# Quarters of the values projection placed between the groups of transposed rows, in a four-layer attention and feed-forward kernel

## The chip, the cores and the metric

The kernel runs on one core of a Trainium2 chip. The metric is device time in microseconds (us) of one execution. The time before is 1589.06 us, the median of three runs (1588.38 to 1591.19).

## What is computed

The input is 2048 rows of 640 numbers. Two kinds of layers alternate, twice each: sliding-window attention (32 heads of 20, a window of 256 rows) and a feed-forward layer with a squared ReLU.

```python
x = x + _A_ref(_layernorm(x, axis=-1), A_wqkv, A_wo)
x = x + _B_ref(_layernorm(x, axis=-1), B_w1, B_b1, B_w2, B_b2)
x = x + _A_ref(_layernorm(x, axis=-1), A_wqkv, A_wo)
x = x + _B_ref(_layernorm(x, axis=-1), B_w1, B_b1, B_w2, B_b2)

# in _A_ref: H = 32, Dh = 20, W = 256
scores = jnp.einsum("bhqd,bhkd->bhqk", q, k) * (Dh ** -0.5)
mask = (idx[:, None] - idx[None, :] >= 0) & (idx[:, None] - idx[None, :] < W)
p = _softmax(jnp.where(mask[None, None], scores, -1e9), axis=-1)
o = jnp.einsum("bhqk,bhkd->bhqd", p, v)          # then @ wo
# in _B_ref: h = max(x @ w1 + b1, 0) ** 2, out = h @ w2 + b2
```

## The kernel before

**Units.** The 2048 rows are cut into 8 groups of 256; a *unit* u is one group in one attention-and-feed-forward pair, so there are 16 units. A unit needs its normalised rows transposed (`yT`), the projections to queries and keys (`stage_qk`) and to values (`stage_v`), eight *quads* of four heads each of attention, the output projection (`stage_o`) and the feed-forward part (`stage_f`). Numbers are carried as two float16 halves, so that a product takes three matmuls; `mm3` at L330 issues nearly all of the dense ones.

**Normalising and transposing.** `ln_load(u)` loads two blocks of 128 rows into `xt` (L431, on SyncE's queue) and normalises them: statistics on VectorE (L356, L360, L361), a power on GpSimd (L367), the scaling on VectorE (L369). For units 0 to 2 `ln_t(u)` then transposes the blocks on TensorE: `split_t` takes a block as two groups, of three and of two transposes (L404), each group into one PSUM bank, from which ScalarE takes the high half (L390) and VectorE the low half (L391). The values are projected in four quarters (two blocks by two halves of the columns), each of 15 matmuls of 128x320 (L330), evicted by ScalarE (L597).

**PSUM.** Dense accumulators, transposes and the values' products (`pv`) share two banks (`mm_tile`, tag `mm`, two buffers), so that the third such piece of work has to wait until one of the two before it has been evicted. The scores have six banks of their own (`bb`).

**Queries and keys.** Ten groups of 15 matmuls of 128x256 (L330), five for the queries, then five for the keys. They are evicted in pairs by ScalarE (L523) and VectorE (L526) into one buffer `qd`, written to DRAM when queries or keys are complete (L559, L561), and read back in another layout into `qt` and `kt` (L565). There is one `qd` for units 1 and 2: the keys' first eviction waits until the write of the queries has landed.

**A quad of attention.** I write m0 to m7 for unit 0's eight quads of maximum scores (L686; from unit 1 on L671, m8 and up), whose row maxima VectorE takes (L652). After each two quads TensorE transposes the maxima (L739), VectorE splits them (L744, L745) and SyncE's queue writes them as rows of `qt` with four DMAs (L707); I call the four such steps r0, r1, r2, r3. Then come s0, s1, ...: the scores once more with the maxima in them (L783, from s9 on L775), whose exponentials ScalarE takes (L797) and GpSimd masks (L812, L816); and v0, v1, ...: the product with the values (L846), copied out (L858) and written to DRAM (L863).

**What sets the order.** Every engine's order is fixed when the program is built: `tc.manual_schedule` takes instructions as they are recorded. TensorE's order is that of the code; work for the other engines is posted with an estimated cost and a rank (`post`, a lower `prio` first) and recorded by `pump` when a clock of estimates says that it can start. In unit 0 `flow` goes through a list of m, r, s and v steps; wherever the next step's inputs are not yet there by the estimates, it takes pieces of dense work from the generator `ahead_all`, which holds the projections of units 0 to 2 that come ahead of the loop. The estimates know when a row maximum or an exponential is ready; that `qd` is still being read by a DMA they do not know. `convert` turns weights into two halves on ScalarE (L259) and VectorE (L260); the weights are loaded by DMAs that ScalarE issues (L288, L297, L312).

```python
    def split_t(y, dst, m, job, made, bb=None):
        for k, (c0, n) in enumerate(((0, 3), (3, 2))):
                tr, jobs = mm_tile([P, 4, P], "tr")
    def ahead_all():
        yield from stage_qk(0)
    todo = [("m", n) for n in range(GQ)] + [("r", 0)] + [("m", n) for n in range(GQ, LEAD)]
    for n in range(NQ):
        todo += [("s", n)] + ([("r", n + LEAD - GQ)] if n % GQ == 1 else []) + [("m", n + LEAD), ("v", n)]
    flow(todo, rest)
```

Of the kernel before, what the change touches and what calls it, by code (L numbers as in the profile page):

```python
# [16 lines left out]
P = 128  # L17
# [28 lines left out]
def kernel(ctx: ExitStack, tc: tile.TileContext, x, wqkv, wo, w1, b1, w2, b2, out):  # L46
# [86 lines left out]
    def post(eng, cost, fn, *deps, wait=0.0, prio=1, **kw):  # L133

        j = Job(eng, cost, fn, [d for d in deps if d is not None], now[0] + wait, prio, **kw)
        k = len(pend)
        while k and pend[k - 1].prio > prio:
            k -= 1
        pend.insert(k, j)
        return j  # L140
# [5 lines left out]
    def dma(fn, size, *deps, n=1, cost=450.0, prio=1, **kw):  # L146

        return post("S", n * cost, fn, *deps, prio=prio, size=size, **kw)
# [18 lines left out]
    def need(*js):  # L167

        for j in js:
            while j.end is None:  # L170
                pass_time()
            now[0] = max(now[0], j.end)
# [55 lines left out]
    def mm_tile(shape, name):  # L228


        while len(banks2) > 1:
            empty = [b for b in banks2 if b and all(j.end is not None for j in b)]
            if empty:
                b = min(empty, key=lambda b: max(j.end for j in b))
                now[0] = max(now[0], max(j.end for j in b) + LAT)
                banks2.remove(b)
            else:
                pass_time()
        t = ps.tile(shape, F32, name=name, tag="mm", bufs=2)
        banks2.append([])  # L240
        return t, banks2[-1]
# [80 lines left out]
    def mm3(acc, lhs, rhs, nk, ns, then=None, whole=0):  # L322

        k, t = 0, 0.0
        terms = ((0, 0), (0, 1), (1, 0))
        if whole:
            terms = [[t] for t in (terms if whole == 1 else terms[::2] + terms[1:2])]
        for c, part in ([(c, part) for part in terms for c in range(nk)] if whole else [(c, terms) for c in range(nk)]):
            for a, b in part:
                nc.tensor.matmul(acc, lhs(a, c), rhs(b, c), start=(k == 0), stop=(k == 3 * nk - 1))  # L330
                k += 1
                t += ns
                if t >= STEP and k < 3 * nk:
                    yield t
                    t = 0.0
        if then is not None:
            then(t)
        yield t
# [10 lines left out]
    def layernorm(src, y, *deps, prio=2):  # L349

        box = {}

        def stats(i):
            if i == 0:
                box["st"] = sb.tile([P, 2, 6], F32, name="bst", bufs=2)
            nc.vector.bn_stats(box["st"][:, i, :], src[:, i * HD:(i + 1) * HD])  # L356

        def var():
            box["mv"] = mv = sb.tile([P, 4], F32, name="bmv", bufs=2)
            nc.vector.bn_aggr(mv[:, 0:2], box["st"])  # L360
            nc.vector.tensor_scalar(mv[:, 2:3], mv[:, 1:2], 1e-5, YS ** -2, op0=ALU.add, op1=ALU.mult)  # L361

        j = None
        for i in range(2):
            j = post("D", 455, lambda i=i: stats(i), j, *(deps[i:i + 1] or deps), prio=prio)
        j = post("D", 400, var, j, prio=prio)
        j = post("G", 520, lambda: nc.gpsimd.tensor_tensor(box["mv"][:, 3:4], box["mv"][:, 2:3], neghalf,  # L367
                                                                   op=ALU.pow), j, prio=prio)
        j = post("D", 576, lambda: nc.vector.tensor_scalar(y, src, box["mv"][:, 0:1], box["mv"][:, 3:4],  # L369
                                                           op0=ALU.subtract, op1=ALU.mult), j, prio=prio)  # L370
        return j

    def halves(tile):

        return lambda a, c, n, m: tile[:, a, c:c + n, m]

    def pieces_of(*tiles):

        return lambda a, c, n, m: tiles[2 * a + c // 3][:, c % 3:c % 3 + n, m]

    ALL = slice(0, T)

    def split_t(y, dst, m, job, made, bb=None):


        yield Want(job, bank=False)
        need(job)

        def out(tr, jobs, c0, n, wait):
            j = post("A", 170 * n, lambda: nc.scalar.copy(dst(0, c0, n, m), tr[:, :n]), wait=wait, prio=0)  # L390
            j = post("D", 170 * n, lambda: nc.vector.tensor_sub(dst(1, c0, n, m), tr[:, :n], dst(0, c0, n, m)), j,  # L391
                     prio=0)
            jobs.append(j)
            made.append(j)

        parts = []
        for k, (c0, n) in enumerate(((0, 3), (3, 2))):
            if bb is not None:
                tr, jobs = bb[:, k].rearrange("p (c n) -> p c n", n=P), bbjobs
            else:  # L400
                yield Want()
                tr, jobs = mm_tile([P, 4, P], "tr")
            for c in range(n):
                nc.tensor.transpose(tr[:, c, :], y[:, (c0 + c) * P:(c0 + c + 1) * P], ident)  # L404
            parts.append((tr, jobs, c0, n, 117 * n if bb is None else 117 * KC))
            if bb is None:
                out(*parts.pop())
                yield 117 * n
        if parts:
            for p in parts:  # L410
                out(*p)
            yield 117 * KC
# [3 lines left out]
    def xsrc(l, b):  # L416
        return x_rows[b * P:(b + 1) * P, :] if l == 0 else xs[b]
# [7 lines left out]
    def ln_load(u, *deps, prio=2):  # L425

        l, g = divmod(u, NG)
        ys = []
        for i in range(2):
            xt = sb.tile([P, D], F32, name="xt", tag="xt", bufs=2)  # L430
            load = dma(lambda xt=xt, i=i: nc.sync.dma_start(xt, xsrc(l, 2 * g + i)), P * D * 4, *deps, prio=min(prio, 1))  # L431
            ys.append((xt, layernorm(xt, xt, load, prio=prio)))
        lns[u] = ys

    def ln_t(u, yT=None):
        ys = lns.pop(u)
        if u == 0:
            yT = pieces_of(sb.tile([P, 3, T], F16, name="yT", tag="yT", bufs=1), sb.tile([P, 2, T], F16, name="rs", bufs=1),
                           *[sb.tile([P, n, T], F16, name="x1", bufs=2) for n in (3, 2)])
        else:  # L440
            yT = halves(sb.tile([P, 2, KC, T], F16, name="yT", tag="yT", bufs=1) if yT is None else yT)
        yTs[u], pre[u] = yT, []
        bb = banks() if u == 0 else (None, None)
        for i in range(2):
            yield from split_t(ys[i][0], yT, slice(i * P, (i + 1) * P), ys[i][1], pre[u], bb[i])

    def cross(ys, dst, room, prio=2):

# [34 lines left out]
    pre = {}  # L483
# [100 lines left out]
    def stage_v(u, which=range(4)):  # L584
        yT = yTs[u]
        for i in range(2):
            if u == 2:
                yield Want(sums[i], bank=False)
            vt = vts[(2 * u + i) % 6][0]
            for h in range(2):  # L590
                if 2 * i + h not in which:
                    continue
                yield Want()
                acc, jobs = mm_tile([P, 2 * T], "acc")
                need(*[wqj[c] for c in range((2 * D + h * HD) // P, (2 * D + (h + 1) * HD - 1) // P + 1)])
                def out(vt=vt, acc=acc, h=h):
                    nc.scalar.activation(vt[:, h * NP:(h + 1) * NP, 0:DH],  # L597
                                                 acc[:, :HD].rearrange("p (h d) -> p h d", d=DH),
                                                 AF.Copy, scale=1.0 / (YS * WS))

                yield from mm3(acc[:, :HD], lambda a, k: yT(a, k, 1, slice(i * P, (i + 1) * P)),
                               lambda b, k: wq_s[:, b, k, 2 * D + h * HD:2 * D + (h + 1) * HD], KC, 136,
                               lambda wait: jobs.append(post("A", 320, out, wait=wait, prio=urgency["out"])))
# [11 lines left out]
    def banks():  # L615
        need(*bbjobs)
        bbjobs.clear()
        return bb6
# [252 lines left out]
    x1s, ys, y2s = {}, {}, {}  # L871
# [357 lines left out]
    place = kts[2].rearrange("p a n -> p (a n)")[:, :2 * KC * T].rearrange("p (a c n) -> p a c n", a=2, n=T)  # L1229

    def ahead_all():
        yield from stage_qk(0)
        yield from stage_v(0, range(2))
        yield from ln_t(1, place)
        ln_load(2)
        yield from stage_v(0, range(2, 4))
        yield from stage_qk(1)
        yield from ln_t(2)
        yield from stage_v(1)
        gate2.end = now[0]  # L1240
        yield from stage_qk(2)
        yield from stage_v(2)
# [65 lines left out]
```

## Time and profile before

| | |
|---|---|
| median of three runs | 1589.06 us |
| the profiled execution's own time | 1596.68 us |
| its span, first to last instruction | 1595.0 us |
| TensorE busy | 1561.6 us (98%) |
| VectorE busy | 983.5 us (62%) |
| ScalarE busy | 734.0 us (46%) |
| GpSimd busy | 601.1 us (38%) |
| mean granted TensorE clock | 0.993 |

The profile is of one execution, which took 7.62 us more than the median of the runs that were timed without it; 1.68 us of its time lie outside the span. PE is TensorE's matmuls, PEld its weight loads, DVE VectorE, ACT ScalarE, POOL GpSimd, SP SyncE; ACTq and SPq are the instructions with which ScalarE and SyncE issue DMAs. In a timeline a row reads: start in us, length in us, engine, line, operation, out<-in, count, and in brackets the idle time ahead of it and what ended that. PEclk is the granted clock of TensorE as a share of full speed. Line numbers are those of the kernel before; in the changed kernel all from L409 on are higher by two.

### The profile page before, as it was taken

The numbers are of one execution on the slowest core, as the hardware profiler recorded it, in microseconds if no ns is written. First come the engines' busy times: TensorE is split into PE (matmuls) and PEld (weight loads), VectorE is DVE, ScalarE is ACT, GpSimd is POOL, SyncE is SP. The second block draws the span as 40 slices with busy tenths as digits, with TensorE's granted clock in tenths as the row PEclk, the third lists the DMA queues.
The fourth block names the chain that finished last, engine by engine and source line by source line (L and its number), as shares of the span: only waits on it lengthen the run. The fifth ranks groups of instructions, "written<-read, shape, count | busy, mean of one in ns | idle before, by whom it ended". The sixth has DMA issues, their size and how long they took to land.

```text
span 1595.0 us, 52003 instructions
## 1 busy us (share of the span) xinstructions
PE 1561.6 (98%) x21302; PEld 1169.1 (73%) x21302; DVE 983.5 (62%) x3253; ACT 734.0 (46%) x1593; POOL 601.1 (38%) x1291
## 2 busy tenths in 40 slices
PE   8889999999999999999999999999999999999999
PEld 7666767777777777777777777777777777776767
DVE  8777655666656667565466656557665665756441
ACT  4455535345454444535444453444545345454522
POOL 1233525335253343524324252442535235353512
PEclk9998999999999999999999999999999999999999
DMA  9754254453434524344352534535344353431120
GB/s 282 193 164 117 63 120 82 98 119 67 118 90 101 113 54 119 86 120 94 88 130 65 122 87 112 101 78 119 70 123 83 97 122 64 110 83 57 29 67 17
DMA packets 243207, 160.41 MB, mean 101 GB/s; under 512 B 91160, under 2 KB 226712, under 8 KB 242968
## 3 DMA queue, kind: packets, MB, share of 16 engines
q1 hardware_dynamic: 236600, 147.58, 38.5%
q10 hardware_dynamic: 6368, 9.50, 2.1%
q8 instruction: 167, 2.74, 0.7%
q14 instruction: 72, 0.59, 0.1%
HBM read 84.68 MB, written 52.95 MB: 86 GB/s over the span
## 4 chain that ended last, share of the span: by engine, by line
PE 91%; DVE 3%; DMA 2%; ACT 2%; issue 1%; POOL 0%; SPq 0%; ACTq 0%; DVEq 0%; POOLq 0%
PE acc L330 70%; PE pv L846 11%; PE bb L671 5%; PE bb L775 5%; ACT pt L797 1%; DVE bb L652 1%; DMA qt<-mT 1%; DVE wq_s L260 1%; DMA od<-o 0%; PE bb L783 0%; DMA ov<-o 0%; PE bb L686 0%; DVE qd L526 0%; DMA qk<-qd 0%; DVE mx L652 0%
## 5 line engine op out<-in xcount | busy, mean ns | idle before, releaser
L797 ACT ACTIVATE pt<-bb 128x512 f32<-128x512 f32 (+1 forms) x736 | 376.2, 600 | 224.3 <-PE bb L775 192.9
L652 DVE CUSTOM_DVE_ANT_0 bb<-bb,maskq 128x320 f32<-128x320 f32 x896 | 409.1, 523 | 96.1 <-PE bb L671 89.5
L812 POOL TENSOR_SCALAR_AFFINE_SELECT pt<-pt 128x256 f32<-128x256 f32 x448 | 189.3, 425 | 560.4 <-ACT pt L797 548.1
L330 PE MATMUL acc<-y,w_s 128*128 128x256 f16 x2832 | 326.9, 273 | 1.5 <-ACT y L390 1.4
L330 PE MATMUL acc<-w_s,hh 128*128 128x320 f16 x2304 | 326.2, 299 | 0.0
L330 PEld LDWEIGHTS <-w_s 128*128 128x128 f16 x2880 | 276.5, 98 | 52.8 <-issue 17.0
L330 PEld LDWEIGHTS <-hh 128*128 128x128 f16 x2304 | 220.5, 98 | 98.4 <-issue 11.5
L330 PEld LDWEIGHTS <-wq_s 128*128 128x128 f16 x2400 | 229.7, 98 | 46.1 <-issue 14.2
L330 PE MATMUL acc<-yT,wq_s 128*128 128x256 f16 x2160 | 253.2, 273 | 2.8 <-DVE qd L526 1.2
L816 POOL TENSOR_SCALAR_AFFINE_SELECT pt<-pt 128x256 f32<-128x256 f32 x512 | 214.8, 442 | 93.1 <-ACT pt L797 91.6
L1037 DVE TENSOR_TENSOR hh<-r,hh 128x256 f16<-128x256 f32 x192 | 94.7, 513 | 212.4 <-ACT hh L1034 205.0
L846 PE MATMUL pv<-pt,vt 128*32 128x128 f32 (+1 forms) x3840 | 193.9, 333 | 0.7 <-POOL pt L816 0.6
L1031 POOL TENSOR_TENSOR r<-r 128x256 f32<-128x256 f32 x192 | 114.5, 618 | 168.2 <-ACT r L1027 166.1
L858 ACT COPY ot<-pv 128x256 f32<-128x256 f32 x128 | 47.7, 373 | 272.9 <-PE pv L846 269.0
L330 PE MATMUL acc<-wo_s,od 128*128 128x320 f16 x960 | 141.2, 303 | 3.2 <-ACT od L929 2.9
L652 DVE DVE_READ_ACCUMULATOR2_ANT mx<- 128x1 f32 x1024 | 142.8, 139 | 0.0
L846 PEld LDWEIGHTS pv<-pt,vt 128*32 128x32 f32 x3840 | 106.6, 111 | 42.9 <-POOL pt L816 7.1
L330 PE MATMUL acc<-wq_s,yT 128*128 128x320 f16 x864 | 129.0, 300 | 1.6 <-DVE qd L526 0.6
L330 PEld LDWEIGHTS <-od 128*128 128x128 f16 x960 | 92.1, 99 | 49.3 <-issue 6.8
L1027 ACT ACTIVATE r<-acc,b1s 128x256 f32<-128x256 f32 x192 | 80.7, 472 | 95.2 <-PE acc L330 94.3
L330 PEld LDWEIGHTS <-yT 128*128 128x128 f16 x864 | 82.5, 98 | 39.0 <-issue 7.4
L367 POOL TENSOR_TENSOR bmv<-bmv,neghalf 128x1 f32<-128x1 f32 x64 | 44.4, 701 | 139.7 <-DVE bmv L361 139.3
(105 smaller groups left out, 1269.5 us busy)
## 6 DMA issues: line engine op xcount, KB each, us to landing
qt<-qk SPq DMA_DIRECT2D x30, 480.0 KB
kt<-qk SPq DMA_DIRECT2D x30, 480.0 KB
qk<-qd SPq DMA_DIRECT2D x17, 640.0 KB
o<-ot SPq DMA_DIRECT2D x256, 42.0 KB
od<-o SPq DMA_DIRECT2D x14, 640.0 KB
qk<-yl SPq DMA_DIRECT2D x13, 640.0 KB
qk<-qd SPq DMA_DIRECT2D x17, 320.0 KB
xt<-in_A_x_dram SPq DMA_DIRECT2D x16, 320.0 KB
```

The source lines that it names most:

```text
L330: nc.tensor.matmul(acc, lhs(a, c), rhs(b, c), start=(k == 0), stop=(k == 3 * nk - 1))
L652: nc.vector.tensor_tensor_reduce(out=v, in0=v, in1=mask, scale=1.0, scalar=-3.0e38, op0=ALU.add, op1=ALU.max, accum_out=accum[e, w]),
L671: nc.tensor.matmul(flat[e][rows, o:o + b - a], qt[r, p, i * P + 64 * h:i * P + 64 * (h + 1)], kt[r, p, a + to:b + to], start=True, stop=Tr ...
L775: nc.tensor.matmul(bb[e][rows, k, o + a:o + b], kt[r, 2 * qd + j, ko + 64 * h:ko + 64 * (h + 1)], qt[r, 2 * qd + j, q0 * P + a:q0 * P + b] ...
L797: nc.scalar.activation(box["pt"][:, :o], bb[e][:, k, :o], AF.Exp, scale=SCALE / (QS * QS))
L812: nc.gpsimd.affine_select(out=m, in_=m, pattern=[[0, 2], [-1, P]], compare_op=ALU.is_gt, fill=0.0, base=0, channel_multiplier=1)
L816: nc.gpsimd.affine_select(out=m, in_=m, pattern=[[0, 2], [1, P]], compare_op=ALU.is_ge, fill=0.0, base=0, channel_multiplier=-1)
L846: nc.tensor.matmul(pv[32 * jj:32 * (jj + 1), q0 * P:(q0 + qn) * P], vf[:, c:c + 32], pj[:, j, :], start=(k == 0), stop=(k == len(steps) - ...
L858: nc.scalar.copy(ot[:, qd % 2], pv)
L1027: nc.scalar.activation(box["r"], acc[:, f, :], AF.Relu, bias=b1s[:, f0 + f:f0 + f + 1], scale=1.0 / (YS * WS))
L1031: nc.gpsimd.tensor_tensor(box["r"], box["r"], box["r"], op=ALU.mult)
L1037: nc.vector.tensor_sub(hh[:, 1, f, :], box["r"], hh[:, 0, f, :])
```

## The change

Within `split_t` a piece of other work may now follow each group of transposes. Unit 0's values: one quarter ahead of unit 1's transposes, the other three after the first, second and third group of them (before: two quarters, all four groups, two quarters). Unit 1's four quarters: one after each of unit 2's four groups (before: all groups, then all quarters). Unit 2's normalisation, `ln_load(2)`, is asked for after the last quarter of unit 0 instead of in the middle, and with rank 1, that of the row maxima and exponentials (`urgency["turn"]`), where it had rank 2.

```diff
-    def split_t(y, dst, m, job, made, bb=None):
+    def split_t(y, dst, m, job, made, bb=None, between=()):
...
             if bb is None:
                 out(*parts.pop())
                 yield 117 * n
+                for g in between[k:k + 1]:
+                    yield from g
...
-    def ln_t(u, yT=None):
+    def ln_t(u, yT=None, between=()):
...
-            yield from split_t(ys[i][0], yT, slice(i * P, (i + 1) * P), ys[i][1], pre[u], bb[i])
+            yield from split_t(ys[i][0], yT, slice(i * P, (i + 1) * P), ys[i][1], pre[u], bb[i], between[2 * i:2 * i + 2])
...
         yield from stage_qk(0)
-        yield from stage_v(0, range(2))
-        yield from ln_t(1, place)
-        ln_load(2)
-        yield from stage_v(0, range(2, 4))
+        yield from stage_v(0, range(1))
+        yield from ln_t(1, place, [stage_v(0, [k]) for k in (1, 2, 3)])
+        ln_load(2, prio=1)
         yield from stage_qk(1)
-        yield from ln_t(2)
-        yield from stage_v(1)
+        yield from ln_t(2, None, [stage_v(1, [k]) for k in range(4)])
         gate2.end = now[0]
```

Since `flow` takes dense work by its clock of estimates, other steps move too. The first piece is of TensorE, at unit 1's transposes: one piece of the difference ahead of m0, and one where before all ten transposes stood (acc<-wq_s are quarters of unit 0's values, tr<-ident the transposes).

```order
 L330 LDWEIGHTS x_156
 L330 MATMUL acc<-wq_s,x_156 128x320
+L404 MATMUL tr<-ident,xt 128x128 x3
 L330 LDWEIGHTS yT
 L330 MATMUL acc<-wq_s,yT 128x320
...
 L330 LDWEIGHTS x_156
 L330 MATMUL acc<-wq_s,x_156 128x320
-L404 MATMUL tr<-ident,xt 128x128 x10
```

The ten transposes of unit 1 are no longer in a row; its first three stand after one quarter, ahead of m0.

On VectorE, at m3, the first quad of maxima after s0 (L652, printed as ISA), there stood before:

```order
L361 TENSOR_SCALAR bmv<-bmv 128x1
L652 ISA bb_133,mx<-bb_133,maskw 128x128
L652 ISA mx 128x1
L652 ISA bb_134,mx<-bb_134,maskw 128x128
L652 ISA mx 128x1
L652 ISA bb_133,mx<-bb_133,maskw 128x256
L652 ISA mx 128x1
L652 ISA bb_134,mx<-bb_134,maskw 128x256
```

and now:

```order
L654 ISA bb_134,mx<-bb_134,maskw 128x128
L654 ISA mx 128x1
L356 BN_STATS bst<-xt 128x6
L654 ISA bb_133,mx<-bb_133,maskw 128x256
L654 ISA mx 128x1
L356 BN_STATS bst<-xt 128x6
L360 BN_AGGR bmv<-bst 128x2
L361 TENSOR_SCALAR bmv<-bmv 128x1
L356 BN_STATS bst<-xt 128x6
```

Unit 2's statistics stood ahead of m3's maxima and now stand among them. By the estimates the maxima are then ready later, and `flow` takes 65 of unit 1's query and key matmuls between v0 and s1 instead of 25, and 30 between v1 and s2 instead of 40.

On ScalarE the rows from the second weight load L297 on were these before (L523, in the changed kernel L525, are the evictions of queries and keys to `qd`: the last two of the queries, then the first of the keys; L797 are the exponentials of s1):

```order
L297 DMA w_s<-in_B_w_dram 128x5x256 [waits DMAHW0_49]
L523 ACTIVATE qd<-acc 128x2x256 [waits PE_49]
L523 ACTIVATE qd<-acc 128x256 [waits PE_49]
L797 ACTIVATE pt<-bb_133 128x512 [waits DVE_49,PE_49]
L797 ACTIVATE pt<-bb_134 128x512 [waits DVE_49,PE_49,Pool_49]
L797 ACTIVATE pt<-bb_133 128x256 [waits Pool_49]
L797 ACTIVATE pt<-bb_134 128x256 [waits Pool_49]
L259 ACTIVATE wo_s<-w_s 128x640 [waits DMAHW6_49,DMAHW4_49]
L259 ACTIVATE wo_s<-w_s 128x640
L858 COPY ot<-pv 128x256 [waits PE_49]
L259 ACTIVATE wo_s<-w_s 128x640 x3
L523 ACTIVATE qd<-acc 128x2x256 [waits DMAHW1_49,DMAHW2_49,DVE_49,PE_49]
```

and are these now:

```order
L297 DMA w_s<-in_B_w_dram 128x5x256 [waits DMAHW0_49]
L525 ACTIVATE qd<-acc 128x2x256 [waits PE_49]
L525 ACTIVATE qd<-acc 128x256 [waits PE_49]
L297 DMA w_s<-in_B_w_dram 128x5x256 [waits DMAHW1_49]
L259 ACTIVATE wo_s<-w_s 128x640 [waits DMAHW6_49]
L259 ACTIVATE wo_s<-w_s 128x640
L525 ACTIVATE qd<-acc 128x2x256 [waits DMAHW2_49,DMAHW3_49,DVE_49,PE_49]
L259 ACTIVATE wo_s<-w_s 128x640
L799 ACTIVATE pt<-bb_133 128x512 [waits PE_49]
L799 ACTIVATE pt<-bb_134 128x512 [waits DVE_49,PE_49,Pool_49]
L799 ACTIVATE pt<-bb_133 128x256 [waits Pool_49]
L799 ACTIVATE pt<-bb_134 128x256 [waits Pool_49]
```

The keys' first eviction, with its wait for DMAs, has moved from behind s1's exponentials to ahead of them, and a third load of `w1` (L297) has moved up to stand ahead of it.

## Prediction

> **What bounds the kernel now.** I read the page first, for the busy times.
>
> ```profile
> PE 1561.6 (98%) x21302; PEld 1169.1 (73%) x21302; DVE 983.5 (62%) x3253; ACT 734.0 (46%) x1593; POOL 601.1 (38%) x1291
> ```
>
> TensorE is busy for 98% of the span: what the kernel can gain is TensorE's idle time, and time at a low clock. Two sets of windows say where these lie (busy us and counts by engine, then granted clock, DMA share, GB/s).
>
> ```profile
> 30.00:150.00 120.00, 105.79 (x1190) 72.41 (x1191) 89.23 (x316) 60.12 (x126) 30.86 (x62) 0.93 0.68 178
> 150.00:1595.00 1445.00, 1429.35 (x19908) 1073.40 (x19900) 867.41 (x2876) 658.15 (x1440) 565.11 (x1215) 1.00 0.38 90
> 35.63:39.04 3.41, 3.41 (x14) 1.92 (x13) 2.67 (x17) 0.00 (x0) 0.00 (x0) 0.50 0.99 262
> 80.00:83.41 3.41, 3.41 (x18) 1.71 (x14) 0.00 (x0) 1.64 (x4) 1.54 (x4) 0.50 0.79 141
> 117.55:127.79 10.24, 7.96 (x52) 4.14 (x45) 8.76 (x28) 2.05 (x5) 1.02 (x3) 0.50 1.10 237
> ```
>
> From 30 to 150 us, where the edited work lies, TensorE idles 14.2 us (120 less 105.79) and runs at half clock in three stretches, each behind idle time; a busy stretch of 3.41 us at 0.50 costs 1.7 us. TensorE's order there changes only up to about 160 us (the order of the two programs agrees from then on), so the question is how much later or earlier TensorE gets through that part. Its timeline names the waits (s0, r1 and so on as above).
>
> ```profile
> 32.60 0.44 PE L404 MATMUL tr<-ident,xt 128*128 128x128 f32 x2 [0.20 <-ACT vt L597]
> 33.77 0.77 PE L404 MATMUL tr<-ident,xt 128*128 128x128 f32 x5 [0.73 <-DVE kt L391]
> 35.48 0.57 PE L330 MATMUL acc<-wq_s,yT 128*128 128x320 f16 x2 [0.50 <-DVE kt L391]
> 42.03 3.98 PE L330 MATMUL acc<-kt,wq_s 128*128 128x256 f16 x35
> 47.08 0.49 PE L783 MATMUL bb<-qt,kt 62*128 62x256 f16 x7 [0.86 <-DMA qt<-mT]
> 50.47 2.90 PE L330 MATMUL acc<-kt,wq_s 128*128 128x256 f16 x25
> 67.76 0.44 PE L404 MATMUL tr<-ident,xt 128*128 128x128 f32 x2 [0.55 <-DVE qd L526]
> 68.44 1.12 PE L404 MATMUL tr<-ident,xt 128*128 128x128 f32 x5 [0.24 <-DVE yT L391]
> 70.56 0.70 PE L330 MATMUL acc<-wq_s,kt 128*128 128x320 f16 x4 [1.00 <-DVE yT L391]
> 79.27 0.27 PE L783 MATMUL bb<-qt,kt 62*128 62x256 f16 x1 [1.84 <-DMA o<-ot]
> 79.84 0.67 PE L783 MATMUL bb<-qt,kt 62*128 62x256 f16 x7 [0.30 <-DMA qt<-mT]
> 88.44 1.25 PE L330 MATMUL acc<-yT,wq_s 128*128 128x256 f16 x10 [0.53 <-ACT vt L597]
> 105.50 1.64 PE L846 MATMUL pv<-pt,vt 128*32 128x256 f32 x16
> 108.32 3.98 PE L330 MATMUL acc<-yT,wq_s 128*128 128x256 f16 x35 [1.19 <-DVE qd L526]
> 122.33 7.01 PE L330 MATMUL acc<-wo_s,od 128*128 128x320 f16 x30 [2.28 <-ACT od L929]
> ```
>
> The rows at 32.60 to 35.48 are unit 1's transposes: three waits of 1.43 us in all, for evictions of the transposes and values, then the half clock of 35.63. Those at 67.76 to 70.56 are unit 2's, 1.79 us. s0 waits 0.86 us and s4 2.14 us for rows of maxima that DMAs carry; behind s4 stands the second half clock. The row at 105.50 is v7, unit 0's last product. From its end (107.14) to the output projection (122.33) runs a chain by DRAM and VectorE of 15.2 us, which this edit leaves as it is; TensorE is early for it and waits. So the time of v7 sets the rest, and I add up what TensorE loses ahead of v7.
>
> Before, that is 1.43 + 1.7 (half clock) + 0.86 + 1.79 + 2.14 + 1.7 (half clock) + 0.53 = 10.15 us.
>
> **The change part by part.** No matmul, transpose or DMA is added or removed; each term is a wait.
>
> *Unit 1's quarters between its groups.* A group now follows a quarter and the next quarter a group, so each needs the bank of the quarter just ended. The row at 32.60 prices that, 0.20 us; three such come to 0.6. The last group stands right ahead of unit 1's queries, which need all four low halves: L390 and L391 on two transposes, with part of m2's maxima ahead of them on VectorE, for 1.0 to 1.3 us by these rows:
>
> ```profile
> 33.08 0.37 ACT L390 CAST kt<-tr 128x256 f16<-128x256 f32 x1 [0.16 <-PE tr L404]
> 68.64 0.42 DVE L391 TENSOR_TENSOR yT<-tr,yT 128x256 f16<-128x256 f32 x1 [0.26 <-ACT yT L390]
> ```
>
> That is 1.75 us, and I count no half clock, since the longest of these waits, 1.3 us at most, is less than the 1.43 us that stood ahead of 35.63. The queries (42.03 before) start 1.4 us earlier.
>
> *s0.* r0's maxima were split at 40.78 and s0 went on at 47.08, 6.3 us later.
>
> ```profile
> 40.50 0.28 DVE L745 SCALAR_TENSOR_TENSOR mT<-tr,mT 16x128 f16<-16x128 f32 x1
> 36.06 1.34 SPq L431 DMA_DIRECT2D xt<-in_A_x_dram  x2
> 75.40 1.00 SPq L565 DMA_DIRECT2D kt<-qk  x2
> 76.50 2.92 SPq L863 DMA_DIRECT2D o<-ot  x4
> ```
>
> Now the split comes 1.4 us earlier, five query matmuls fewer (0.5 us) stand ahead of s0, and the two loads L431 stand behind the four row DMAs instead of ahead of them. At an unchanged 6.3 us s0 waits 1.6 us; without the two loads' share, nothing. I take 0.8 us, about as before.
>
> *Keys' eviction behind the queries' write.* This is where I expect the loss. Before, the queries end with the 25 matmuls at 50.47, and s1, r1, m4 and v1 stand between them and the end of the keys' first pair. Now 65 matmuls run without a break: 30 end the queries, 30 more fill the keys' first accumulator, five start the next; then s1, and r1, whose transpose needs a bank. One bank is in use, the other waits for the keys' first eviction, and that for the queries' write to leave `qd`. What this costs is shown by unit 2, where the same wait already binds.
>
> ```profile
> 100.98 0.38 ACT L523 ACTIVATE qd<-acc 128x256 f16<-128x256 f32 x1 [0.41 <-PE acc L330]
> 101.40 0.42 DVE L526 SCALAR_TENSOR_TENSOR qd<-acc,qd 128x256 f16<-128x256 f32 x1 [0.18 <-ACT qd L523]
> 101.85 0.39 SPq L559 DMA_DIRECT2D qk<-qd  x1
> 106.95 0.60 ACT L523 ACTIVATE qd<-acc 128x512 f16<-128x512 f32 x1 [1.57 <-DMA qk<-qd]
> 107.58 0.69 DVE L526 SCALAR_TENSOR_TENSOR qd<-acc,qd 128x512 f16<-128x512 f32 x1 [1.91 <-ACT qd L523]
> 59.31 0.60 ACT L523 ACTIVATE qd<-acc 128x512 f16<-128x512 f32 x1
> 47.71 0.41 ACTq L297 DMA_DIRECT2D w_s<-in_B_w_dram  x1
> 50.61 0.38 ACTq L297 DMA_DIRECT2D w_s<-in_B_w_dram  x1
> 69.66 0.37 ACTq L297 DMA_DIRECT2D w_s<-in_B_w_dram  x1
> 71.97 0.38 ACTq L297 DMA_DIRECT2D w_s<-in_B_w_dram  x1
> w_s<-in_B_w_dram ACTq DMA_DIRECT2D x1, 640.0 KB
> 48.80:54.80 6.00, 5.89 (x68) 4.17 (x67) 4.61 (x22) 2.54 (x7) 2.19 (x6) 1.00 0.74 223
> 55.20:58.70 3.50, 3.50 (x45) 2.56 (x44) 2.64 (x16) 3.35 (x8) 1.23 (x3) 1.00 0.91 284
> ```
>
> From the queries' last eviction (100.98) to TensorE's next matmul in that bank (108.32) it is 7.34 us. In that time TensorE has 35 matmuls (3.98 us at 42.03) and s1 (0.49 us at 47.08), 4.5 us. It waits 2.9 us at least at r1. On VectorE the queries' last L526 also stands behind a scaling and a statistic of unit 2 (up to 0.6 us), and the third weight load of 640 KB is now issued just ahead of the write; the window at 55.20, the write by itself, moved 284 GB/s, at which 640 KB take 2.3 us. So 2.9 to 5.8 us; I take 4.0. Idle time of that length has stood ahead of half clock at 80.00, where 1.84 + 0.30 us were enough, so I add one stretch, 1.7 us (none to two: 0 to 3.4). [...]
>
> *Unit 2's quarters and groups.* Of the 1.79 us I leave 0.5 (0.3 to 1.0): its changes of bank at 0.20 us each, partly under quads that stand between. *s4.* r2's rows had two weight loads ahead of them (L297 at 69.66 and 71.97); one has moved up. Of 2.14 us I leave 0.5 (0 to 1.3) and no half clock. *m8.* On SyncE's queue the read of unit 1's keys (L565 at 75.40) now stands behind v3's four writes (2.92 us at 76.50), which wait for v3; m8 needs the keys. 0.5 us (0 to 1.7). *m10.* ScalarE now has unit 2's first key eviction between s7's exponentials, and it waits for the write as at 106.95 (1.57 us): m10 and v7 behind it lose 0.5 to 1.7 us, say 1.2. The 1.19 us at 108.32 that it replaces lay behind v7, in the chain, and is no credit. *The 0.53 us at 88.44* goes with the quarter that it stood behind.
>
> After: 1.75 + 0.8 + 4.0 + 1.7 + 0.5 + 0.5 + 0.5 + 1.2 = 10.95 us. Against 10.15 that is +0.8; five matmuls more (0.55 us) now stand ahead of v7, since 40 instead of 45 of the projections are left behind it: +1.35 us. At the low ends it is 5.3 us (−4.3 with the 0.55), at the high ends 18.4 us (+8.8). Behind v7 the same work follows the same chain. The profiled execution took 1596.68 us, 7.62 more than the median of the runs shown; it would take 1598.0, and the median 1590.4.
>
> **The rivals.**
> *Faster: the write is out of the way in time.* If the 65 matmuls and s1 cover the write, or `qd`'s wait is not the last, r1's 4.0 and its half clock go: 5.25 us against 10.15, with the 0.55 us −4.35 us, 1584.7. For it: before, at 59.31, the same eviction came without a wait. Against it: 7.34 us against 4.5 us of cover in this trace.
> *Slower: the write shares the DMA engines with the third weight load.* Then r1 waits 5.0 us or more, two half stretches follow (3.4), s4 loses 1.3 and m8 1.7: 1.75 + 0.8 + 5.0 + 3.4 + 0.5 + 1.3 + 1.7 + 1.2 = 15.65, +6.05 us, 1595.1. It decides from a wait of about 4.5 us at r1 with two half stretches. For it: the load now stands right ahead of the write. Against it: the window at 48.80 holds two such loads (issued at 47.71 and 50.61) at a DMA share of 0.74, so there is room. [...]
> That the edit does not do what it says is ruled out by the order above.
>
> **How the numbers follow.** This kernel's runs spread so that 0.2%, 3.2 us, is about what can be told from no change. My forecast, +1.35 us, is inside: 0.46. The faster rival has 0.19, the slower 0.35, as more of the terms can grow than shrink. The range takes in both rivals and most of the bounds: 1585.0 to 1597.0 us.
>
> **What would show it.** Right: a wait of 3 to 6 us ahead of r1 (L741 in the changed kernel) near 56 us, ended by VectorE's eviction of `qd`, with ScalarE's L525 waiting for the write; half clock behind it; waits of about 0.2 us beside the transposes; no half clock near 36 us. Wrong: no wait at r1, or v7 more than 3.2 us from 105.50, or a new wait behind 160 us.

## The result and the profile after

| | before | changed |
|---|---|---|
| median, measured side by side on one chip | 1589.51 us (6 runs, 1587.34 to 1592.12) | 1597.05 us (6 runs, 1594.68 to 1600.84) |
| ratio to before, 95% interval | | 1.0050 (1.0033 to 1.0066) |
| profiled execution: own time, span | 1596.68, 1595.0 us | 1596.14, 1594.4 us |

The changed kernel is slower by 7.5 us, where I had forecast 1.35 us, no change that can be told. 1597.05 lies at the upper end of the range, just outside it. The profiled execution of the changed kernel was forecast at 1598.0 us and took 1596.14; this time it is an ordinary one, 0.9 us below the median of its runs.

TensorE's timeline of the changed kernel, with the rows that answer to the terms of the sum:

```profile
29.85 0.43 PE L330 MATMUL acc<-wq_s,yT 128*128 128x320 f16 x2 [0.20 <-ACT vt L599]
33.11 0.43 PE L330 MATMUL acc<-wq_s,yT 128*128 128x320 f16 x2 [0.31 <-ACT vt L599]
36.38 0.43 PE L330 MATMUL acc<-wq_s,yT 128*128 128x320 f16 x2 [0.20 <-ACT vt L599]
44.08 0.28 PE L785 MATMUL bb<-qt,kt 62*128 62x256 f16 x1 [1.20 <-DMA qt<-mT]
44.60 0.49 PE L785 MATMUL bb<-qt,kt 62*128 62x256 f16 x7 [0.24 <-DMA qt<-mT]
47.99 7.27 PE L330 MATMUL acc<-kt,wq_s 128*128 128x256 f16 x65
60.54 0.38 PE L741 MATMUL tr<-ident,mx 128*16 128x128 f32 x1 [4.84 <-DVE qd L528]
68.94 1.79 PE L330 MATMUL acc<-wq_s,kt 128*128 128x320 f16 x12 [0.27 <-DVE qd L528]
76.92 0.55 PE L404 MATMUL tr<-ident,xt 128*128 128x128 f32 x3 [0.53 <-ACT vt L599]
81.74 1.25 PE L330 MATMUL acc<-wq_s,kt 128*128 128x320 f16 x8 [0.31 <-ACT vt L599]
90.76 0.71 PE L330 MATMUL acc<-yT,wq_s 128*128 128x256 f16 x5 [0.68 <-DVE mT L747]
104.91 0.70 PE L330 MATMUL acc<-yT,wq_s 128*128 128x256 f16 x5 [0.68 <-DVE mT L747]
106.75 0.75 PE L673 MATMUL bb<-kt,qt 60*64 60x128 f16 x35 [0.96 <-ACT pt L799]
107.43 0.88 PE L848 MATMUL pv<-pt,vt 128*32 128x256 f32 x16
122.18 4.09 PE L330 MATMUL acc<-wo_s,od 128*128 128x320 f16 x14 [3.90 <-ACT od L931]
```

The lump of 65 matmuls stands at 47.99, and behind it r1 (60.54) waits 4.84 us for VectorE's eviction of the keys. v7 starts at 107.43; the forecast had it at 105.50 + 1.35 = 106.85. ScalarE's, VectorE's and SyncE's timelines show what r1 waits for:

```profile
51.47 0.38 ACT L525 ACTIVATE qd<-acc 128x256 f16<-128x256 f32 x1 [1.04 <-PE acc L330]
51.48 0.38 ACTq L297 DMA_DIRECT2D w_s<-in_B_w_dram  x1
52.43 0.38 SPq L561 DMA_DIRECT2D qk<-qd  x1
59.16 0.60 ACT L525 ACTIVATE qd<-acc 128x512 f16<-128x512 f32 x1 [5.90 <-DMA qk<-qd]
59.79 0.69 DVE L528 SCALAR_TENSOR_TENSOR qd<-acc,qd 128x512 f16<-128x512 f32 x1 [4.27 <-ACT qd L525]
```

The queries' write is issued at 52.43, right behind a weight load; the keys' first eviction can start only at 59.16, 6.73 us later. The windows show half clock from the end of the wait on, 1.5 us (2.96 busy us at 0.50), and again at the output projection:

```profile
60.10:63.50 3.40, 2.96 (x19) 1.87 (x19) 2.41 (x5) 3.05 (x7) 2.49 (x3) 0.50 0.37 100
121.60:128.40 6.80, 6.22 (x23) 3.28 (x24) 6.14 (x17) 2.17 (x5) 0.00 (x0) 0.50 1.13 222
```

So the changed side came out nearly as forecast, and yet the kernel is slower. The question was whether the error lies in the *before* side of the sum. **Theory A:** the loss is the wait that the lump brings to light, and the sum set it against waits and half clocks of an execution that was not typical of before. The rivals are written with the runs.

### The profile page after: what moved, and what is told of

It is laid out like the page before. It is cut to its first block, busy times and chain, and to the rows that moved or that the text cites. A ratio compares the mean times of both kernels' runs of the same rounds, so it can differ in the third digit from the quotient of the medians.

```text
span 1594.4 us, 52008 instructions
## 1 busy us (share of the span) xinstructions
PE 1557.6 (98%) x21302; PEld 1166.9 (73%) x21302; DVE 985.0 (62%) x3253; ACT 733.5 (46%) x1593; POOL 598.6 (38%) x1291
## 4 chain that ended last, share of the span: by engine, by line
PE 92%; DVE 3%; ACT 2%; DMA 1%; POOL 1%; issue 1%; SPq 0%; ACTq 0%; POOLq 0%; DVEq 0%
PE acc L330 71%; PE pv L848 11%; PE bb L777 5%; PE bb L673 5%; ACT pt L799 1%; DMA qk<-qd 1%; DVE bb L654 1%; DVE wq_s L260 1%; PE bb L688 0%; PE bb L785 0%; POOL pt L818 0%; POOL pt L814 0%; DVE qd L528 0%; POOL r L1033 0%; DVE bst L356 0%
```

## The experiments

All were timed in five rounds against before on the same chip. Three such groups of four ran; before's medians in them were 1591.06, 1590.90 and 1590.26 us.

**The kernel before once more**, no edit.

> The kernel before, unchanged, profiled a second time. Theory A (the waits of the prediction's sum are right, but the execution profiled before was an unlucky one: 1596.68 us against a median of 1589.5, with 24 us of half clock): the span is near 1588 us, the idle times of TensorE are those of the first profile within 1 us in all (28.3 us), and the half clock is well under 24 us, 10 to 15. Theory B (the executions differ by something other than the clock): the span is shorter with the same half clock, and some idle times are gone.

Measured: 1590.55 us, ratio 0.9997 (0.9988 to 1.0006); this profiled execution took 1589.59 us. First its windows, where the first profile had 0.93 and twice 0.50, then TensorE's timeline:

```profile
30.00:150.00 120.00, 107.47 (x1280) 75.32 (x1278) 93.83 (x333) 62.97 (x134) 32.28 (x65) 0.99 0.69 178
35.63:39.04 3.41, 3.08 (x24) 1.98 (x25) 2.96 (x19) 0.44 (x1) 0.00 (x0) 1.00 1.16 236
80.00:83.41 3.41, 3.35 (x36) 1.95 (x29) 3.41 (x16) 1.58 (x4) 0.00 (x0) 1.00 0.93 231
```

```profile
34.03 0.77 PE L404 MATMUL tr<-ident,xt 128*128 128x128 f32 x5 [0.73 <-DVE kt L391]
35.73 0.43 PE L330 MATMUL acc<-wq_s,yT 128*128 128x320 f16 x2 [0.49 <-DVE kt L391]
...
45.90 0.49 PE L783 MATMUL bb<-qt,kt 62*128 62x256 f16 x7 [0.87 <-DMA qt<-mT]
66.57 0.44 PE L404 MATMUL tr<-ident,xt 128*128 128x128 f32 x2 [0.56 <-DVE qd L526]
...
69.37 0.70 PE L330 MATMUL acc<-wq_s,kt 128*128 128x320 f16 x4 [1.00 <-DVE yT L391]
76.83 0.49 PE L783 MATMUL bb<-qt,kt 62*128 62x256 f16 x7 [0.23 <-DMA qt<-mT]
83.95 1.25 PE L330 MATMUL acc<-yT,wq_s 128*128 128x256 f16 x10 [0.53 <-ACT vt L597]
101.01 1.62 PE L846 MATMUL pv<-pt,vt 128*32 128x256 f32 x16
116.56 0.44 PE L330 MATMUL acc<-wo_s,od 128*128 128x320 f16 x2 [2.29 <-ACT od L929]
```

The waits at unit 1's transposes are the same, 0.73 and 0.49 us, but no half clock follows; s4 (76.83) waits 0.23 us instead of 2.14, and there is no half clock at 80. v7 starts at 101.01 instead of 105.50, and the execution is 7 us shorter than the first one. The control below, whose instructions have the same order, agrees: v7 starts at 100.34 and no half clock stands ahead of it. Theory A's half clock came true, but not its idle times within 1 us: between 30 and 150 us they fall from 14.2 to 12.5 us, about what s4's late rows had cost, so a part of theory B holds too. What I had set against the changed kernel's losses belonged to one execution.

**The changed kernel, unit 1's keys in memory of their own.** The order of all instructions stays.

```diff
+                elif j and u == 1:
+                    qd = hraw[:, KC * T:2 * KC * T].bitcast(F16).rearrange("p (c a n) -> p c a n", a=2, n=T)
```

> The changed kernel with one thing undone: unit 1's keys are evicted to a buffer of their own, so that they no longer wait for the queries' write. The order on every engine is as in the changed kernel. Theory A: the wait of 4.84 us ahead of r1 goes, and the half clock behind it; 4.8 to 6.5 us less than the changed kernel, 1590 to 1592 us, ratio to the kernel before 1.001 (0.999 to 1.003). Theory C (the loss is not that wait but what comes behind it, such as m8, m10 or the output projection): at most 1.5 us less, ratio 1.004 to 1.005.

Measured: 1593.11 us, 1.0013 (1.0005 to 1.0022). TensorE's timeline:

```profile
56.06 0.28 PE L743 MATMUL tr<-ident,mx 128*16 128x128 f32 x1 [0.48 <-DVE stg L530]
102.73 0.88 PE L850 MATMUL pv<-pt,vt 128*32 128x256 f32 x16
```

r1 waits 0.48 us, and v7 starts 4.7 us earlier than in the changed kernel. (The ratio lies in the range that theory A gave, the 1593.11 us lie 1.1 us above it.) From 1.0050 to 1.0013 is 5.9 us of before's time; from 1.0034, the changed kernel's second comparison (below), it is 3.3 us. By either, most of the loss is this one wait and its half clock; the remaining 0.13% is not.

**Its control: the kernel before with the same edit.**

> The kernel before, with unit 1's keys evicted into memory of their own; no instruction changes its place. It is the control of the run in which the changed kernel got the same. Theory A (the edit's loss is the wait that the lump of 65 matmuls brings to light): before, the keys' first eviction came after the write of the queries had landed, so the separate buffer changes nothing here: 0.9990 to 1.0010 of before. Rival B (the separate buffer makes any version of this kernel faster, so the changed kernel's gain with it says nothing of the lump): 0.9965 or less.

Measured: 1590.35 us, 0.9994 (0.9985 to 1.0002). The separate buffer by itself can't be told from no change, so in the changed kernel it removes what the edit added. Theory A held, rival B fell.

**The third weight load held back** until the queries' write has landed.

```diff
-                st, ..., gate,
+                st, ..., gate3 if f0 == 2 else gate,
...
+        if (u, j) == (1, 0):
+            wrote.gates.append(gate3)
```

(The first two loads of `w2` wait for `gate3` too; in the changed kernel the first of them is issued at 59.79, after the keys' eviction has begun.)

> The changed kernel, but the third load of w1 (and the first of w2) may not be issued until the write of unit 1's queries has landed; TensorE's order is the same until behind r1. Theory A (7.34 us from the queries' last eviction to the freed bank, without other traffic, against 4.5 us of cover): r1 still waits about 3 us. Rival C (the write is slow because the 640 KB just ahead of it share its engines): the 6.7 us from issue to landing fall to about 5, and r1's 4.84 us to about 3.2; if more than 1.5 us go, the load was the larger part of what the forecast missed. Rival D (the write's own length, whatever else is loaded): r1 keeps 4.5 us or more. In time: 1.0035 to 1.0050 of before under A and D, 1.0025 to 1.0045 under C, since loads that come later may delay s4 and the feed-forward weights.

Measured: 1594.90 us, 1.0025 (1.0015 to 1.0034). From the timelines of SyncE, ScalarE and TensorE, and a window:

```profile
52.57 0.38 SPq L561 DMA_DIRECT2D qk<-qd  x1
57.40 0.60 ACT L525 ACTIVATE qd<-acc 128x512 f16<-128x512 f32 x1 [4.16 <-DMA qk<-qd]
58.77 0.28 PE L743 MATMUL tr<-ident,mx 128*16 128x128 f32 x1 [2.95 <-DVE qd L528]
```

```profile
58.77:62.17 3.40, 3.15 (x29) 1.76 (x29) 3.05 (x11) 2.62 (x6) 2.89 (x4) 1.00 0.01 2
```

From the write's issue to the eviction it is 4.83 us instead of 6.73: 1.9 us of r1's wait go when 640 KB of weights no longer move beside the write (rival C; I had written 1.5 us as its point of decision). The other 2.95 us are the write's own length against 4.5 us of cover, the lower bound of the forecast (2.9). Behind this shorter wait the clock stayed at 1.00.

**Both remedies at once.**

> The changed kernel with both remedies, unit 1's keys evicted into memory of their own and the third weight load held back until the queries' write has landed. If the load's sharing costs only through the keys' wait: no more is won than by the separate buffer alone, 1.0005 to 1.0022 of before. If the load also delays others (rows of maxima, m8): 0.9990 to 1.0005.

Measured: 1592.64 us, 1.0010 (1.0001 to 1.0019), not told apart from the separate buffer alone. Here the load beside the write cost nothing that these runs can tell besides the keys' wait.

**The planner told of the write.** The estimates learn that the keys' eviction follows the landing of the write:

```diff
-post("A", 60 + 212 * n, high, wait=wait, prio=pr)
+post("A", 60 + 212 * n, high, *([left_of[u, 0]] if j and u in (1, 2) and (u, 0) in left_of else []), wait=wait, prio=pr)
...
+        left_of[u, j] = wrote
```

> The changed kernel, with the estimates told that the keys' first eviction of units 1 and 2 cannot start before the queries' write has landed; the lump of 65 matmuls stays, but on ScalarE the exponentials of s1 now stand ahead of the keys' eviction, and behind r1 TensorE takes m4 and v1 instead of ten matmuls. Theory A: the bank is still held by the eviction, so r1 keeps waiting 4 to 5 us; order on ScalarE alone cures nothing: 1.0035 or more of before. Rival H (the loss is what is queued behind the waiting eviction on ScalarE, not the bank): the wait at r1 goes, 1.0015 or less.

Measured: 1600.94 us, 1.0060 (1.0046 to 1.0073). Timelines of ScalarE, VectorE and TensorE:

```profile
57.78 3.88 ACT L259 ACTIVATE w_s<-w_s 128x640 f16<-128x640 f32 x6
61.54 0.61 ACT L525 ACTIVATE qd<-acc 128x512 f16<-128x512 f32 x1
58.72 4.90 DVE L260 SCALAR_TENSOR_TENSOR w_s<-w_s 128x640 f16<-128x640 f32 x6
63.55 0.68 DVE L528 SCALAR_TENSOR_TENSOR qd<-acc,qd 128x512 f16<-128x512 f32 x1
64.28 0.38 PE L743 MATMUL tr<-ident,mx 128*16 128x128 f32 x1 [8.65 <-DVE qd L528]
```

Rival H's forecast, that the wait goes, failed: s1's exponentials ran ahead of the eviction, from 55.66 on, and r1 waited longer. The run is no clean test of order on ScalarE, though. I had missed that a later date for the eviction lets the planner fill the gap with weight conversions, which the eviction then stands behind. On SyncE the read of the queries that waits for the write goes out at 58.57, so the write has landed by then; the eviction starts 3.0 us later on ScalarE, behind the conversions, and VectorE's half later still. So here the bank is held by what stands in the two engines' order as well, and the wait grew to 8.65 us.

**Unit 2's normalisation back to rank 2**, all else as changed: `ln_load(2)` in place of `ln_load(2, prio=1)`.

> The quarters between the groups as in the changed kernel, but unit 2's normalisation with its old rank 2, so that 15 instead of 65 matmuls stand between v0 and s1. Theory A: no wait of more than 0.5 us ahead of r1, 1589 to 1592 us, ratio 1.000 to 1.002. Theory D (the quarters themselves cost, by bank waits and by steps that bunch up later): 1594 us or more, ratio over 1.003.

Measured: 1601.88 us, 1.0062 (1.0049 to 1.0076), a miss for theory A; the time is that of theory D, the cause in the main another. Timelines of ScalarE and TensorE:

```profile
62.72 0.60 ACT L525 ACTIVATE qd<-acc 128x512 f16<-128x512 f32 x1 [4.11 <-DMA qk<-qd]
63.65 1.07 PE L688 MATMUL bb<-kt,qt 60*128 60x128 f16 x8 [3.87 <-ACT pt L799]
```

There is no lump ahead of r1, but the keys' eviction waits for the write all the same, now with exponentials queued behind it on ScalarE, and it is a quad of maxima that finds no bank. The wait had only changed its victim. The lump is thus one way to meet it, not its cause. Half clock goes on here behind the wait: the window from 60.10 to 63.50 has 0.75, and 20 matmuls of the projection take 3.58 us at 66.09, where 20 took 2.36 us at 57.42. Smaller waits follow (the longest ahead of v7 1.63 us, at 84.39), so that the loss is larger than in the changed kernel.

**The quarters for unit 1 alone, rank 2.** `ln_t(2)` and `stage_v(1)` as in the kernel before.

> The changed kernel with the quarters between unit 1's groups alone, and unit 2's normalisation at its old rank 2; unit 2's groups and unit 1's values stand as before. TensorE then takes 15 instead of 65 query and key matmuls between v0 and s1. Theory A: the keys' eviction comes after the write has landed, r1 waits less than 1 us, and the 1.2 us of waits that the quarters take out at unit 1's transposes show in the end: 0.9985 to 1.0005 of before. Rival E (any early start of unit 1's queries moves the key eviction ahead of the write, as in the run with both units' quarters at rank 2, where m waited 3.87 us): a wait of 3 us or more between 55 and 70 us, 1.0030 or more.

Measured: 1602.51 us, 1.0073 (1.0061 to 1.0086). TensorE's timeline:

```profile
63.73 0.76 PE L688 MATMUL bb<-kt,qt 60*128 60x128 f16 x8 [4.18 <-ACT pt L799]
82.60 1.30 PE L404 MATMUL tr<-ident,xt 128*128 128x128 f32 x5 [6.36 <-DVE xt L369]
```

Rival E held: the same wait at a quad of maxima, and 6.36 us for unit 2's rows, which at rank 2 are normalised too late for transposes that come earlier. Rank 1 avoids that second wait.

**The quarters for unit 2 alone**, unit 1 and the normalisation as before.

```diff
-        yield from ln_t(2)
-        yield from stage_v(1)
+        yield from ln_t(2, None, [stage_v(1, [k]) for k in range(4)])
```

> The kernel before with unit 1's quarters alone placed between unit 2's groups of transposes; the first block and the rank are as before. Theory A: the waits of 1.79 us at unit 2's transposes fall to about 0.5, no wait ahead of r1, ratio 0.998 to 1.000. Theory D: the steps that bunch up behind cost more than is saved, ratio over 1.001.

Measured: 1593.11 us, 1.0012 (1.0003 to 1.0021). ScalarE's and TensorE's timelines:

```profile
102.33 0.60 ACT L525 ACTIVATE qd<-acc 128x512 f16<-128x512 f32 x1 [3.69 <-DMA qk<-qd]
103.70 6.19 PE L330 MATMUL acc<-yT,wq_s 128*128 128x256 f16 x40 [2.64 <-DVE qd L528]
```

The waits at unit 2's transposes shrink, and what they gave comes back at unit 2's own keys: the wait for the write is 3.69 us there, and TensorE loses 2.64 us where it lost 0.71 in the repeated run of before. The 40 matmuls behind it take 6.19 us, where 40 take 4.57 us in the repeated run (at 93.54): at a clock of 0.50 that is half clock for about 3.2 us, an estimate from these two rows. Theory A's range (0.998 to 1.000) was missed; theory D's forecast, over 1.001, came true.

**The rank alone, and unit 1 with the keys apart.** In the first, before's `ln_load(2)` gets `prio=1` at its old place; the second is the changed kernel without unit 2's quarters and with the separate buffer. In both orders the values of some rows differ from the reference's, and I did not trace which step is behind it; so their times are read for the order of work only, and neither is a version to use.

> The kernel before with one word changed: unit 2's normalisation asked for at rank 1 instead of 2, at its old place; all transposes and quarters stand as before. TensorE takes 35 instead of 25 query and key matmuls between v0 and s1, and 15 instead of 10 behind r1. Theory A: no lump of 65, so no long wait at r1 (less than 1 us): 0.9990 to 1.0020 of before. Rival F (the rank alone delays the maxima and costs the most of the 0.5%): 1.0030 or more.

> The changed kernel without the quarters between unit 2's groups (all seven remaining transposes of unit 2 follow s3, then unit 1's values), rank 1 kept, and with unit 1's keys evicted into memory of their own. It asks whether the rest of the loss, 0.13% with the keys apart, belongs to unit 2's quarters, which cost 0.12% by themselves. If so: no waits of 0.7 us at unit 1's last values beside r3 and r4, 0.9985 to 1.0008 of before, and it is the first version that could beat it. If not (what is left belongs to unit 1's part and the rank): 1.0010 to 1.0030.

Measured: 1594.56 us, 1.0020 (1.0011 to 1.0030), and 1591.51 us, 1.0003 (0.9994 to 1.0012). The rank alone has no wait at r1, but four of 0.71 to 1.70 us at unit 2's transposes and one of 2.12 us at r4; rival F, 1.0030 or more, did not come true. Without unit 2's quarters the rest of the loss can't be told from nothing, which agrees with the 0.12% that they cost alone; but this order has 2.98 us at 102.57 and other waits that the changed kernel has not, so it does not single out unit 2's quarters, and the cause of the last 0.13% stays open.

**The changed kernel once more.**

> The changed kernel, unchanged. Its first profile is one execution, as the forecast's profile of before was. Theory A: the 4.8 us at r1 is in this execution too, between 4.3 and 5.4 us, with half clock behind it, and v7 starts near 107.4 us; half clock elsewhere may differ. Rival G (this profile too was an unlucky one, and most executions wait about 3 us): less than 4 us at r1. Time 1.0033 to 1.0066 of before.

Measured: 1596.59 us, 1.0034 (1.0021 to 1.0046). TensorE's timeline and a window:

```profile
61.03 0.28 PE L741 MATMUL tr<-ident,mx 128*16 128x128 f32 x1 [4.94 <-DVE qd L528]
107.91 0.89 PE L848 MATMUL pv<-pt,vt 128*32 128x256 f32 x16
```

```profile
61.30:64.70 3.40, 3.40 (x27) 1.87 (x28) 2.52 (x9) 2.35 (x6) 2.90 (x4) 0.50 0.32 94
```

The wait, its half clock and v7's time are those of the first profile: on the changed side the execution was typical, and rival G fell.

No version that computes the reference beat the kernel before; the best, before with the separate buffer, can't be told from it.

## Why the prediction was wrong

The forecast compared two sums of TensorE's losses ahead of v7. Here they stand against the rows above, in us.

| term | before: forecast | before: repeated run | changed: forecast | changed: profile |
|---|---|---|---|---|
| unit 1's transposes | 1.43 | 1.42 | 1.75 | 0.71 |
| half clock at 36 | 1.7 | 0 | 0 | 0 |
| s0 | 0.86 | 0.87 | 0.8 | 1.44 |
| r1 | 0 | 0 | 4.0 | 4.84 |
| half clock behind r1 | 0 | 0 | 1.7 | 1.5 |
| unit 2's transposes | 1.79 | 1.80 | 0.5 | 1.11 |
| s4 | 2.14 | 0.23 | 0.5 | 0 |
| half clock at 80 | 1.7 | 0 | 0 | 0 |
| 0.53 of the last quarter | 0.53 | 0.53 | 0 | 0 |
| m8 | 0 | 0 | 0.5 | 0 |
| bank behind r3 (90.76) | 0 | 0 | 0 | 0.68 |
| bank behind r4 (104.91), m10 | 0 | 0 | 1.2 | 0.68 + 0.96 |
| sum | 10.15 | 4.85 | 10.95 | 11.92 |

(The 1.42 us hold 0.20 us, and the 1.80 us 0.24 us, of waits not shown. A wait of 0.22 us at r0, at 38.70 of the repeated run alone, is left out.)

**The failed step is the sum for before.** It took two half clocks (1.7 + 1.7) and s4's 2.14 us from one execution as the kernel's own. In the repeated run they are 0, 0 and 0.23: the sum is 5.3 us too high. The prediction had the warning before it, that the execution took 7.62 us more than the median, and used it wrongly, as a constant that both kernels carry: 1598.0 less 7.62 gave 1590.4. The execution's excess lay largely inside the terms that I compared. With the forecast's own changed side against the repeated run, 10.95 − 4.85 + 0.55 is +6.65 us; the two comparisons of the medians measured 7.5 and 6.3 us.

**The mechanism was right.** r1 waits for VectorE's eviction, that for ScalarE's L525, and that for the queries' write; one stretch of half clock follows. Of the size, 4.84 for 4.0, the load's share was under-estimated: 1.9 us measured, where I had taken about 1.1 above the lower bound for load and VectorE's queue together.

**Smaller terms.** The last low halves of unit 1 cost nothing instead of 1.0 to 1.3 us; s0 waits for its rows 0.6 us longer, unit 2's changes of bank 0.6 longer; m8 loses nothing instead of 0.5; the two waits of 0.68 us behind r3 and r4, each a dense group that needs the bank of transposed maxima which VectorE has not yet read, were not forecast. That all this nearly cancels, 11.92 for 10.95, is luck. From the repeated run of before to the changed kernel v7 moved 6.42 us, against 11.92 − 4.85 + 0.55 = 7.62 by the terms; 1.2 us are not accounted for, of which 0.43 stands already at 10 us, where the same row starts at 10.86 and at 10.43, ahead of the edited work.

**The chain behind v7** is unchanged, as assumed, but shorter than I read it: from v7's end to the output projection 116.56 − 102.63 = 13.9 us in the repeated run, and 122.18 − 108.31 = 13.9 us in the changed kernel.

**The rivals.** The faster one is out. The slower one came near in time (1595.1), but not by its own way: of its r1 ≥ 5.0, two half stretches, s4 1.3 and m8 1.7 the profile has 4.84, one, 0 and 0. (The range was said to take in both rivals; the faster one's 1584.7 us lay 0.3 us below it.) Its premise, that the load beside the write prolongs it, holds: with the load held back r1 waited 2.95 us instead of 4.84. That the two shared DMA engines was not shown.

**What would make it wrong** was badly chosen: v7 stood within 3.2 us of 105.50, so my own sign of failure stayed silent. A test against a position in one profile inherits that profile's accident.

## What to carry to other kernels

Before costing an edit against a profile, check that its execution is an ordinary one: where it is longer than the timed median, the excess lies in some of the rows, and those (here two half clocks of 1.7 us behind short waits, and rows for s4 that were late by 2.14 us once and by 0.23 us in the repeated run) must not be booked as savings. When dense work moves earlier, look at the buffer that its eviction writes to and ask who still reads it; a memory of its own cured most of this loss (1.0050 to 1.0013), where a change of order only passed the wait on (3.87 us at a quad of maxima). A planner that does not know of a wait can be wrong in both directions: told of this one, it filled the time with work that the eviction then stood behind, and r1 waited 8.65 us.

## What the runs showed of the hardware

The same short waits led to half clock in one execution and not in another. 0.73 + 0.49 or 0.50 us at unit 1's transposes: halved in the first profile of before (pairs of matmuls, x2, on 128x320 take 0.74 us from 36.11 on), at full clock in its repeated run, in the control with the keys apart and with unit 2's quarters alone (0.43 us a pair). At m10, waits and clock of the held load's run and of the keys apart, first the rows, then the windows in the same order:

```profile
102.42 0.71 PE L330 MATMUL acc<-yT,wq_s 128*128 128x256 f16 x5 [0.68 <-DVE mT L749]
104.26 0.80 PE L675 MATMUL bb<-kt,qt 60*64 60x128 f16 x35 [0.97 <-ACT pt L801]
```

```profile
100.15 0.70 PE L330 MATMUL acc<-yT,wq_s 128*128 128x256 f16 x5 [0.67 <-DVE mT L749]
102.05 0.75 PE L675 MATMUL bb<-kt,qt 60*64 60x128 f16 x35 [1.02 <-ACT pt L801]
```

```profile
104.80:108.20 3.40, 3.40 (x43) 1.89 (x30) 3.37 (x14) 1.03 (x3) 0.55 (x1) 0.50 0.31 75
```

```profile
102.05:105.45 3.40, 3.40 (x69) 2.69 (x69) 3.40 (x12) 0.37 (x1) 1.09 (x2) 1.00 0.72 225
```

Behind 0.97 us the clock was 0.50, behind 1.02 us it was 1.00. With the waits just ahead of them it was 0.50 behind 0.68 + 0.97 = 1.65 us and 1.00 behind 0.67 + 1.02 = 1.69 us. Behind 2.95 us (the held load at r1) it stayed at 1.00. Near 60 us half clock stood beside or behind each of the longer waits: behind 4.84 and 4.94 us (the changed kernel) the clock was 0.50 for 3.40 us, beside 3.87 us (rank 2) 0.75 on the mean from 60.10 to 63.50; behind 4.18 us (unit 1 alone) 20 matmuls of the projection took 3.69 us, where 20 had taken 2.36; behind 8.65 us (the planner told) r1's transpose took 0.38 us, as in the changed kernel's half stretch, where it takes 0.28 us at full clock. So in these runs half clock came with each wait of 3.87 us or more near 60 us, and with a shorter one only sometimes.

For two executions, the first profile of before and that of the changed kernel, the traces give the edges of the half stretches. In before these start at 35.63 and 80.01 (3.41 us each) and at 117.55 (10.24 us), in the changed kernel at 60.12 (3.41 us) and 121.56 (6.83 us); the starts lie 13, 11 and 18 times 3.413 us apart. Cells of 3.413 us counted on from them have, from about 12 to 163 us, a mean clock of either 0.50 or 1.00, with nothing between. Of 77 such cells at full clock five stood right ahead of half clock, and TensorE was idle in them for 1.43, 2.15, 2.22, 3.28 and 3.42 us; in the other 72 it was idle for 1.39 us at most. That is a count of two executions: the 1.42 us at unit 1's transposes in the repeated run of before had no half clock behind them. The edges lie 1.5 us behind a whole number of cells from the start of the span in one profile and 2.1 us in the other. That a wait's place against the edges decides, as 1.65 and 1.69 us with unequal clocks suggest, is my estimate; the edges were read for these two executions alone. So a stretch behind a wait of 1 to 3 us is best entered as a chance.
